# Moving phi off GpSimd, a four-bank PSUM tile for k^T v and attention, and layer norms in later stages, in a four-layer linear-attention and GLU kernel

## Chip, cores and metric

One NeuronCore of a Trainium2 chip. The metric is the device time of one execution in microseconds (us). Both kernels compute the same outputs. Engines are named as in the profile: PE is TensorE, PEld its weight loads, DVE is VectorE, ACT is ScalarE, POOL is GpSimd, SP is SyncE (here: the queue that issues all DMAs).

## The reference, cut to what matters

```python
def _A_ref(x, wqkv, wo):                       # H = 32 heads of 32
    q, k, v = split_heads(x @ wqkv)            # cut
    phi = lambda t: jnp.where(t > 0, t + 1, jnp.exp(t)) + 1e-6
    pq, pk = phi(q), phi(k)
    kv = jnp.einsum("bhsd,bhse->bhde", pk, v)  # needs all of k, v first
    z  = jnp.einsum("bhsd->bhd", pk)
    num = jnp.einsum("bhqd,bhde->bhqe", pq, kv)
    den = jnp.einsum("bhqd,bhd->bhq", pq, z)[..., None] + 1e-6
    return merge_heads(num / den) @ wo
def _B_ref(x, w_gate, w_up, w_down):
    return ((x @ w_gate) * (x @ w_up)) @ w_down
# x: 2048 x 1024, F = 3584, bf16
x = x + _A_ref(_layernorm(x), ...)   # A0
x = x + _B_ref(_layernorm(x), ...)   # B1
x = x + _A_ref(_layernorm(x), ...)   # A2
x = x + _B_ref(_layernorm(x), ...)   # B3
```

## The kernel before: the parts that matter

The author fixes the order of units; each engine runs its own instructions in that order. A token tile is 128 tokens; four tiles make a group. A layer norm is a *statistics* unit (DVE, then two tiny POOL operations for the reciprocal root), a *normalise* unit (DVE), and a *transpose* unit (eight PE transposes, one ACT copy). `weave(main, fill, first, step)` puts one fill unit after each `step` main units from `first` on, and **appends whatever is left of `fill` at the end**.

```python
def phi(ps, dst):                                   # once per 128x512 tile of k or q
    e = work.tile([P, NB], F32, tag="e", name="e")
    nc.scalar.activation(out=e[:], in_=ps[:], func=ACT.Exp)
    nc.gpsimd.tensor_scalar(out=e[:], in0=e[:], scalar1=1.0, scalar2=1e-6, op0=ALU.min, op1=ALU.add)
    nc.vector.scalar_tensor_tensor(out=dst, in0=ps[:], scalar=1.0 + 1e-6, in1=e[:], op0=ALU.add, op1=ALU.max)

def o_unit(t):                                      # attention of one token tile
    for chunks in BANKS:                            # 3 + 3 + 2 chunks of 128 columns, one bank each
        ps = aux_tile()                             # 3 one-bank buffers
        # ... one 132-column matmul per chunk ...
        nc.vector.tensor_scalar(out=den[:], in0=view[:, :, P:ZW], scalar1=1e-6, scalar2=None, op0=ALU.add)
        nc.vector.reciprocal(out=den[:], in_=den[:])
        nc.vector.tensor_tensor(out=onat..., in0=view[:, :, 0:P]..., in1=den[:]..., op=ALU.mult)

# start of layer A0
do([apply_unit(0), tx(0, 0), stats_unit(2), k_unit(0, 0), apply_unit(1), tx(1, 0), stats_unit(3),
    k_unit(1, 0), apply_unit(2), tx(2, 0), k_unit(2, 0), apply_unit(3), tx(3, 0), k_unit(3, 0)])

# attention and output stage: out_group(g) is, per tile, two output units and the statistics
do(weave([q_unit(2, c) for c in range(KD)], o_group(0), 1, 2))
do(weave([q_unit(3, c) for c in range(KD)], to_group(0), 0, 2))
do(weave(out_group(0), o_group(1) + to_group(1), 0, 1))     # four attention units, then four transposes
do(weave(out_group(1), o_group(2) + to_group(2), 0, 1))
do(weave(out_group(2), o_group(3) + to_group(3), 0, 1))
do(weave(out_group(3), ln0, 0, 1))
```

The kernel splits PSUM into eight one-bank buffers: four for matmuls, three auxiliary ones, one for transposes.

Of the kernel before, what the change touches and what calls it, by code (L numbers as in the profile page):

```python
# [25 lines left out]
def kernel(  # L26
# [22 lines left out]
    FB = F // NB  # L49
    HC = P // 32  # L50
    ZW = P + HC
    CPB = NB // ZW
    BANKS = [list(range(b, min(b + CPB, KD))) for b in range(0, KD, CPB)]

# [3 lines left out]
    small = ctx.enter_context(tc.tile_pool(name="small", bufs=NT + 2))  # L58
# [15 lines left out]
    onat = [H[:, o0 + i * D:o0 + (i + 1) * D] for i in range(4)]  # L74
    oT = [H[:, i * KD * G:(i + 1) * KD * G].rearrange("p (c s) -> p c s", s=G) for i in range(2)]
# [43 lines left out]
    for t in range(TPG):  # L119
        load(X[:, t, :], x_view[:, t, :])  # L120
    load_k(0)
# [22 lines left out]


    stat = {}

    def ln_stats(t):
# [3 lines left out]
        mv = small.tile([P, 2], F32, tag="mv", name="mv")  # L152
# [3 lines left out]
        rstd = small.tile([P, 1], F32, tag="rstd", name="rstd")  # L156
# [30 lines left out]
    def mm_tile():  # L187
        return psum.tile([P, NB], F32, tag="mm", bufs=4, name="ps")

    def aux_tile():  # L190
        return psum.tile([P, NB], F32, tag="aux", bufs=3, name="aux")

    def phi(ps, dst):

        e = work.tile([P, NB], F32, tag="e", name="e")
        nc.scalar.activation(out=e[:], in_=ps[:], func=ACT.Exp)  # L196
        nc.gpsimd.tensor_scalar(out=e[:], in0=e[:], scalar1=1.0, scalar2=1e-6, op0=ALU.min, op1=ALU.add)  # L197
        nc.vector.scalar_tensor_tensor(out=dst, in0=ps[:], scalar=1.0 + 1e-6, in1=e[:], op0=ALU.add, op1=ALU.max)  # L198
# [25 lines left out]
    def kv_unit(t):  # L224

        def run():
            if t == 0:
                acc[:] = [aux_tile() for _ in BANKS]
            for b, chunks in enumerate(BANKS):
                for j, c in enumerate(chunks):  # L230
                    nc.tensor.matmul(out=acc[b][:, j * ZW:(j + 1) * ZW], lhsT=pk[t % 4][:, c * P:(c + 1) * P],  # L231
                                     rhs=vz[t % 4][:, c, :], start=(t == 0 and j == 0),
                                     stop=(t == NT - 1), skip_group_check=True)
            if t == NT - 1:
                for b, chunks in enumerate(BANKS):
                    n = len(chunks)
                    nc.vector.tensor_tensor(
                        out=KVz[:, chunks[0]:chunks[0] + n, :],
                        in0=acc[b][:, 0:n * ZW].rearrange("p (c f) -> p c f", f=ZW),
                        in1=mask[:].unsqueeze(1).to_broadcast([P, n, ZW]), op=ALU.mult)  # L240
        return run
# [11 lines left out]
    def o_unit(t):  # L253

        def run():
            g, tl = t // TPG, t % TPG
            for chunks in BANKS:
                n = len(chunks)
                ps = aux_tile()
                for j, c in enumerate(chunks):  # L260
                    nc.tensor.matmul(out=ps[:, j * ZW:(j + 1) * ZW], lhsT=pqT[g % 3][:, c, tl * P:(tl + 1) * P],
                                     rhs=KVz[:, c, :], start=True, stop=True)
                view = ps[:, 0:n * ZW].rearrange("p (c f) -> p c f", f=ZW)
                den = small.tile([P, n, HC], F32, tag=f"den{n}", name="den")
                nc.vector.tensor_scalar(out=den[:], in0=view[:, :, P:ZW], scalar1=1e-6, scalar2=None, op0=ALU.add)
                nc.vector.reciprocal(out=den[:], in_=den[:])  # L266
                nc.vector.tensor_tensor(  # L267
                    out=onat[tl][:, chunks[0] * P:(chunks[0] + n) * P].rearrange("p (c h e) -> p c h e", c=n, h=HC),
                    in0=view[:, :, 0:P].rearrange("p c (h e) -> p c h e", h=HC),
                    in1=den[:].unsqueeze(3).to_broadcast([P, n, HC, 32]), op=ALU.mult)  # L270
        return run
# [21 lines left out]
    def gu_unit(i, f):  # L293
# [3 lines left out]
        def run():  # L297
# [6 lines left out]
            gs = work.tile([P, NB], F32, tag="e", name="gs")  # L304
# [4 lines left out]
    def d_unit(t, n, last):  # L309
        def run():  # L310
            ps = aux_tile()
# [28 lines left out]

    def ones():
        for i in range(4):
            nc.gpsimd.memset(vz[i][:, :, P:ZW], 1.0)

    def layer_A(li):
        ones()
        if li == 0:
            ln_stats(0)
            ln_stats(1)
            do([apply_unit(0), tx(0, 0), stats_unit(2), k_unit(0, 0), apply_unit(1), tx(1, 0), stats_unit(3),  # L350
                k_unit(1, 0), apply_unit(2), tx(2, 0), k_unit(2, 0), apply_unit(3), tx(3, 0), k_unit(3, 0)])
# [6 lines left out]
            lns = []  # L358
            for t in range(TPG, 2 * TPG):
                lns += [stats_unit(t), apply_unit(t)]  # L360
            do(weave(main, lns + tx_group(1, 1), 0, 1))
        else:
            fill = []
            for t in range(3 * TPG, NT):
                fill += [apply_unit(t), tx(t, 3)]
            do(weave(kv_group(0), fill, 0, 2))

# [3 lines left out]
        def next_ln(g):  # L371
            return stats_apply(g) + tx_group(g, g) if li == 0 else []
# [108 lines left out]
```

## Time and profile before

1807.2 us (median of 4 runs). I cut the profiled run into stages at the issue of marker matmuls in PE's timeline; the *floor* of a stage is its matmul counts times the warm issue times read there: 0.216 us for a 512-column matmul, 0.45 us for eight transposes, 0.47 us for eight 132-column matmuls. *Warm* means matmuls at full clock, *cold* at half; the *granted clock* is what the profile records of it.

| stage | us | floor |
|---|---|---|
| start of A0, to the first v matmul | 51.0 | 16 |
| A0 rest of k, v, half of q ("kvq0") | 155.0 | 137 |
| A0 rest of q, attention, output ("O0") | 131.1 | 99 |
| B1 to its last down-projection | 593.8 | 591 |
| turn: to the first k matmul of A2 | 5.5 | |
| A2 k, v, half of q ("kvq2") | 152.8 | 147 with the turn |
| A2 attention, output ("O2") | 130.6 | 99 |
| B3 | 585.7 | 586 |

The GLU layers run within 3 us of their floor; the loss is in the attention layers. The first lines below are from the page of the kernel before: PE's busy share, the granted clock in 40 equal slices of the span (tenths of full speed), and the chain of work that ended last, where POOL has a share.

```profile
PE 1707.1 (94%) x8535; PEld 804.7 (44%) x8704; DVE 527.6 (29%) x1030; ACT 341.7 (19%) x514; POOL 300.2 (17%) x280
...
PEclk6999998999999999999999999899999999999999
...
PE 83%; POOL 8%; DVE 6%; ACT 1%; issue 1%; DMA 0%; another core or an unknown queue 0%; SPq 0%; ACTq 0%
```

PE's waits of the kernel before (what it waited for, us in total, times, longest) name the culprits: the normalise (`xn`), the division (`aux L261 <- DVE H L267`) and the last step of phi (`L198`; 3.2 us more of it stand before v matmuls), all on DVE.

```profile
PE pt L172 <- DVE xn L165: 32.9, 17, 6.9
PE aux L261 <- DVE H L267: 27.8, 46, 1.3
PE ps L206 <- DVE H L198: 8.3, 4, 3.3
```

The timeline of one tile in the start of the kernel before (start, duration, engine, line, operation; in brackets the idle time before it and what ended it). Exp, POOL, DVE, normalise and transpose follow each other, PE waits 3.9 us, and its eight matmuls take 3.60 us, where eight take 1.89 at full clock:

```profile
20.29 3.60 PE L206 MATMUL ps<-W_74,xT_70 128*128 128x512 bf16 x8 [1.10 <-ACT xT_70 L173]
...
23.93 0.60 ACT L196 ACTIVATE e<-ps 128x512 f32<-128x512 f32 x1 [3.69 <-PE ps L206]
24.61 1.94 POOL L197 TENSOR_SCALAR e<-e 128x512 f32<-128x512 f32 x1 [4.11 <-ACT e L196]
26.59 0.69 DVE L198 SCALAR_TENSOR_TENSOR H<-ps,e 128x512 bf16<-128x512 f32 x1 [7.05 <-POOL e L197]
27.19 0.54 DVE L165 TENSOR_SCALAR xn<-X,mv,rstd 128x1024 bf16<-128x1024 bf16 x1
27.79 1.03 PE L172 MATMUL pt<-ident,xn 128*128 128x128 bf16 x8 [3.90 <-DVE xn L165]
```

And PE in the attention and output stage of the kernel before, where attention units (L261, each three banks) wait for DVE bank by bank:

```profile
245.36 1.89 PE L288 MATMUL ps<-D_79,H 128*128 128x512 bf16 x7
248.56 0.35 PE L261 MATMUL aux<-KVz,D_81 128*128 128x132 bf16 x3 [1.31 <-DVE H L267]
249.49 0.35 PE L261 MATMUL aux<-KVz,D_81 128*128 128x132 bf16 x3 [0.58 <-DVE H L267]
250.25 0.40 PE L261 MATMUL aux<-KVz,D_81 128*128 128x132 bf16 x2 [0.42 <-DVE H L267]
251.78 0.51 PE L261 MATMUL aux<-KVz,D_81 128*128 128x132 bf16 x3 [1.13 <-DVE H L267]
252.71 0.51 PE L261 MATMUL aux<-KVz,D_81 128*128 128x132 bf16 x3 [0.42 <-DVE H L267]
253.48 0.40 PE L261 MATMUL aux<-KVz,D_81 128*128 128x132 bf16 x2 [0.26 <-DVE H L267]
253.68 3.47 PE L288 MATMUL ps<-D_78,H 128*128 128x512 bf16 x8
```

The last line shows the second cost: after that stretch the next eight matmuls take 3.47 us instead of 1.89 (durations include the end of the pipeline), because the granted clock has fallen to half.

### The profile page before, as it was taken

The numbers are of one execution on the slowest core, as the hardware profiler recorded it, in microseconds if no ns is written. First come the engines' busy times: TensorE is split into PE (matmuls) and PEld (weight loads), VectorE is DVE, ScalarE is ACT, GpSimd is POOL, SyncE is SP. The second block draws the span as 40 slices with busy tenths as digits, with TensorE's granted clock in tenths as the row PEclk, the third lists the DMA queues.
The fourth block names the chain that finished last, engine by engine and source line by source line (L and its number), as shares of the span: only waits on it lengthen the run. The fifth ranks groups of instructions, "written<-read, shape, count | busy, mean of one in ns | idle before, by whom it ended". The sixth has DMA issues, their size and how long they took to land.

```text
span 1808.9 us, 20106 instructions
## 1 busy us (share of the span) xinstructions
PE 1707.1 (94%) x8535; PEld 804.7 (44%) x8704; DVE 527.6 (29%) x1030; ACT 341.7 (19%) x514; POOL 300.2 (17%) x280
## 2 busy tenths in 40 slices
PE   4889987999999999999989999789999999999999
PEld 1444444444444444444444444444444444444444
DVE  2333368422211221122122225872211111111111
ACT  1333221221111011012123333112101111110110
POOL 2466641100000000000014677110000000000000
PEclk6999998999999999999999999899999999999999
DMA  8000210544045035124120003008413431440500
GB/s 278 1 1 1 93 47 1 198 151 140 0 143 169 15 106 169 51 90 143 47 94 1 1 10 128 4 10 279 154 61 100 142 105 59 140 145 18 163 23 24
DMA packets 147514, 158.59 MB, mean 88 GB/s; under 512 B 3040, under 2 KB 138208, under 8 KB 147424
## 3 DMA queue, kind: packets, MB, share of 16 engines
q1 hardware_dynamic: 147424, 157.30, 26.6%
q8 instruction: 68, 1.11, 0.3%
q14 instruction: 22, 0.18, 0.0%
HBM read 153.09 MB, written 4.19 MB: 87 GB/s over the span
## 4 chain that ended last, share of the span: by engine, by line
PE 83%; POOL 8%; DVE 6%; ACT 1%; issue 1%; DMA 0%; another core or an unknown queue 0%; SPq 0%; ACTq 0%
PE ps L302 43%; PE aux L314 21%; POOL e L197 8%; PE ps L206 5%; PE ps L288 5%; PE ps L216 5%; PE pt L172 2%; DVE H L267 2%; PE ps L248 1%; DVE st L151 1%; DVE X L280 1%; DVE den L266 1%; PE aux L231 1%; DVE H L198 1%; ACT e L196 1%
## 5 line engine op out<-in xcount | busy, mean ns | idle before, releaser
L306 DVE TENSOR_TENSOR H<-gs,ps 128x512 bf16<-128x512 f32 x224 | 154.0, 687 | 613.7 <-PE ps L302 610.9
L197 POOL TENSOR_SCALAR e<-e 128x512 f32<-128x512 f32 x128 | 245.8, 1920 | 143.4 <-ACT e L196 136.4
L305 ACT COPY gs<-ps 128x512 f32<-128x512 f32 x224 | 131.2, 585 | 731.4 <-PE ps L302 705.6
L314 PEld LDWEIGHTS <-H 128*128 128x128 bf16 x1792 | 174.2, 98 | 207.3
L155 POOL TENSOR_SCALAR ve<-mv 128x1 f32<-128x1 f32 x64 | 15.8, 247 | 773.2 <-DVE mv L153 728.0
L280 DVE TENSOR_TENSOR X<-X,aux 128x512 bf16<-128x512 bf16 x64 | 44.0, 688 | 328.2 <-PE aux L314 312.2
L196 ACT ACTIVATE e<-ps 128x512 f32<-128x512 f32 x128 | 76.4, 597 | 179.9 <-PE ps L206 93.6
L198 DVE SCALAR_TENSOR_TENSOR H<-ps,e 128x512 bf16<-128x512 f32 x64 | 44.3, 692 | 193.4 <-POOL e L197 193.4
L302 PEld LDWEIGHTS <-W_75 128*128 128x128 bf16 x640 | 62.5, 98 | 75.7
L302 PEld LDWEIGHTS <-W_74 128*128 128x128 bf16 x640 | 62.4, 98 | 74.9
L302 PEld LDWEIGHTS <-W_77 128*128 128x128 bf16 x576 | 56.2, 98 | 68.1
L302 PEld LDWEIGHTS <-xT_73 128*128 128x128 bf16 x576 | 56.2, 98 | 68.1
L302 PEld LDWEIGHTS <-xT_72 128*128 128x128 bf16 x576 | 56.1, 98 | 67.1
L302 PEld LDWEIGHTS <-W_76 128*128 128x128 bf16 x576 | 56.0, 98 | 66.4
L151 DVE BATCH_NORM_STATS2 st<-X 128x6 f32<-128x512 bf16 x128 | 81.7, 680 | 3.5 <-DMA X<-in_A_x_dram 3.5
L302 PE MATMUL ps<-xT_71,W_75 128*128 128x512 bf16 x317 | 75.4, 379 | 0.3
L302 PE MATMUL ps<-xT_70,W_75 128*128 128x512 bf16 x318 | 75.5, 379 | 0.2
L288 PEld LDWEIGHTS <-H 128*128 128x128 bf16 x512 | 50.8, 103 | 55.9 <-issue 10.1
L302 PE MATMUL ps<-xT_70,xT_72 128*128 128x512 bf16 x316 | 75.4, 379 | 0.2
L302 PE MATMUL ps<-xT_70,xT_73 128*128 128x512 bf16 x312 | 74.8, 379 | 0.4
L302 PE MATMUL ps<-xT_71,W_76 128*128 128x512 bf16 x314 | 75.0, 379 | 0.3
L302 PE MATMUL ps<-xT_70,W_74 128*128 128x512 bf16 x310 | 74.8, 379 | 0.4
(91 smaller groups left out, 2082.4 us busy)
## 6 DMA issues: line engine op xcount, KB each, us to landing
W_74<-in_B_w_gate_dram SPq DMA_DIRECT2D x20, 1024.0 KB, 5.2
W_75<-in_B_w_up_dram SPq DMA_DIRECT2D x20, 1024.0 KB, 7.0
W_76<-in_B_w_gate_dram SPq DMA_DIRECT2D x18, 1024.0 KB, 5.2
W_77<-in_B_w_up_dram SPq DMA_DIRECT2D x18, 1024.0 KB, 7.2
xT_72<-in_B_w_gate_dram SPq DMA_DIRECT2D x18, 1024.0 KB, 5.2
xT_73<-in_B_w_up_dram SPq DMA_DIRECT2D x18, 1024.0 KB, 7.0
X<-in_A_x_dram SPq DMA_DIRECT2D x16, 256.0 KB, 7.6
out_dram<-X SPq DMA_DIRECT2D x32, 128.0 KB, 1.7
```

The lines of the kernel that those rows point to most:

```text
L151: nc.vector.bn_stats(out=st[:, c, :], in_=X[:, t, c * NB:(c + 1) * NB])
L196: nc.scalar.activation(out=e[:], in_=ps[:], func=ACT.Exp)
L197: nc.gpsimd.tensor_scalar(out=e[:], in0=e[:], scalar1=1.0, scalar2=1e-6, op0=ALU.min, op1=ALU.add)
L198: nc.vector.scalar_tensor_tensor(out=dst, in0=ps[:], scalar=1.0 + 1e-6, in1=e[:], op0=ALU.add, op1=ALU.max)
L206: nc.tensor.matmul(out=ps[:], lhsT=xt[:, k, tl * P:(tl + 1) * P], rhs=wk[n][:, k, :], start=(k == 0), stop=(k == KD - 1))
L216: nc.tensor.matmul(out=ps[:], lhsT=xt[:, k, tl * P:(tl + 1) * P], rhs=wv[n][:, k, :], start=(k == 0), stop=(k == KD - 1))
L280: nc.vector.tensor_tensor(out=X[:, t, n * NB:(n + 1) * NB], in0=X[:, t, n * NB:(n + 1) * NB], in1=ps[:], op=ALU.add)
L288: nc.tensor.matmul(out=ps[:], lhsT=oT[(t // TPG) % 2][:, c, tl * P:(tl + 1) * P], rhs=wo[n][:, c, :], start=(c == 0), stop=(c == KD - 1))
L302: nc.tensor.matmul(out=ps[:], lhsT=w[:, k, j * P:(j + 1) * P], rhs=xT[g % 2][:, k, :], start=(k == 0), stop=(k == KD - 1))
L305: nc.scalar.copy(out=gs[:], in_=gp[:])
L306: nc.vector.tensor_tensor(out=hT[:, f, :], in0=gs[:], in1=up[:], op=ALU.mult)
L314: nc.tensor.matmul(out=ps[:], lhsT=hT[:, f, tl * P:(tl + 1) * P], rhs=wd[f][:, n * NB:(n + 1) * NB], start=(f == 0), stop=(f == KF - 1))
```

## The change

Intent: take POOL out of phi, make the division three DVE operations per tile instead of nine, take layer-norm work out of stages where DVE is busy, shorten the start. PSUM is split anew: three matmul buffers, one four-bank tile, one bank for transposes. Core of the diff (cut):

```diff
-    for t in range(TPG): load(X[:, t, :], x_view[:, t, :])
-    load_k(0)
+    # x tiles 0 and 1, the first k half in two parts, x tiles 2 and 3, then the rest
+    nc.vector.memset(xT[3][:, 0, :], 0.0)
+    for i in range(16):                                # zero matmuls
+        nc.tensor.matmul(out=zps[:], lhsT=xT[3][:, 0, 0:P], rhs=xT[3][:, 0, :], start=True, stop=True)
 def phi(ps, dst):
-        e = work.tile([P, NB], F32, tag="e", name="e")
-        nc.gpsimd.tensor_scalar(out=e[:], in0=e[:], scalar1=1.0, scalar2=1e-6, op0=ALU.min, op1=ALU.add)
+        e = eb[phis[0] % 3]                            # bf16, three buffers
+        nc.vector.tensor_scalar(out=e, in0=e, scalar1=1.0, scalar2=1e-6, op0=ALU.min, op1=ALU.add)
 def o_unit(t):
-            for chunks in BANKS:                       # three banks, nine DVE operations
+            ps = kv_tile()                             # [P, 8, 256] fp32, four banks, one buffer
+            # eight matmuls, then ONE add, ONE reciprocal, ONE multiply over all eight chunks
 def layer_A(li):                                       # start: all norms ahead of the phis on DVE
+            for t in range(TPG):
+                ln_stats(t)
+                if t > 0: ln_apply(t - 1)
+            ln_apply(3)
+            for t in range(TPG):
+                tx(t, 0)()
+                k_unit(t, 0)()
-        return [... (out_unit(t, 0), out_unit(t, 1), stats_unit(t))]
+        return [... (out_unit(t, 0), out_unit(t, 1))]
-        do(weave(out_group(0), o_group(1) + to_group(1), 0, 1))      # o o o o t t t t
+            return [o[0], o[1], tr[0], o[2], tr[1], o[3], tr[2], tr[3]]   # o_fill(g)
+        do(weave(out_group(0), o_fill(1), 0, 1))
+        do(weave(out_group(1), [stats_unit(t) for t in range(TPG)] + o_fill(2), 0, 1))
 def layer_B(li):                                       # statistics come with the norms, in gate/up stages
+            if g == 3 and not last:
+                fill = norm_fill(1, 1, True) + norm_fill(2, 2, True)    # 24 units into 12 places
```

In the k/v/q stage of A0 the norms of the next group now come as four statistics in a row, then normalises and transposes.

More of the change, by code (lines that the diff above doesn't have):

```diff
@@ L49 @@
     FB = F // NB
+    MM = 3
     HC = P // 32
     ZW = P + HC
-    CPB = NB // ZW
-    BANKS = [list(range(b, min(b + CPB, KD))) for b in range(0, KD, CPB)]
+    ZS = NB // 2
     ctx.enter_context(tc.manual_schedule())
@@ L57 @@
     work = ctx.enter_context(tc.tile_pool(name="work", bufs=4))
-    small = ctx.enter_context(tc.tile_pool(name="small", bufs=NT + 2))
+    small = ctx.enter_context(tc.tile_pool(name="small", bufs=4))
     psum = ctx.enter_context(tc.tile_pool(name="psum", bufs=1, space=bass.MemoryType.PSUM))
@@ L74 @@
     onat = [H[:, o0 + i * D:o0 + (i + 1) * D] for i in range(4)]
+    o0 += 4 * D
+    eb = [H[:, o0 + i * NB:o0 + (i + 1) * NB] for i in range(3)]
     oT = [H[:, i * KD * G:(i + 1) * KD * G].rearrange("p (c s) -> p c s", s=G) for i in range(2)]
@@ L117, in load_d @@
             load(Dr[i][:].rearrange("p (f n) -> p f n", n=D), wd_v[:, 4 * i:4 * i + 4, :])
-    for t in range(TPG):
-        load(X[:, t, :], x_view[:, t, :])
-    load_k(0)
+    load(X[:, 0, :], x_view[:, 0, :])
+    load(X[:, 1, :], x_view[:, 1, :])
+    for k in range(0, KD, 4):
+        load(wk[0][:, k:k + 4, :], wqkv_v[:, k:k + 4, D:D + NB])
+    load(X[:, 2, :], x_view[:, 2, :])
+    load(X[:, 3, :], x_view[:, 3, :])
     load_k(1)
@@ L143 @@
     nc.scalar.activation(out=warm[:], in_=mhalf[:], func=ACT.Exp)
+    nc.vector.memset(xT[3][:, 0, :], 0.0)
+    zps = psum.tile([P, NB], F32, tag="mm", bufs=MM, name="zps")
+    for i in range(16):
+        nc.tensor.matmul(out=zps[:], lhsT=xT[3][:, 0, 0:P], rhs=xT[3][:, 0, :], start=True, stop=True)
     stat = {}
@@ L151, in ln_stats @@
             nc.vector.bn_stats(out=st[:, c, :], in_=X[:, t, c * NB:(c + 1) * NB])
-        mv = small.tile([P, 2], F32, tag="mv", name="mv")
+        mv = small.tile([P, 2], F32, tag="mv", bufs=2 * TPG, name="mv")
         nc.vector.bn_aggr(out=mv[:], in_=st[:])
@@ L155, in ln_stats @@
         nc.gpsimd.tensor_scalar(out=ve[:], in0=mv[:, 1:2], scalar1=1e-5, scalar2=None, op0=ALU.add)
-        rstd = small.tile([P, 1], F32, tag="rstd", name="rstd")
+        rstd = small.tile([P, 1], F32, tag="rstd", bufs=2 * TPG, name="rstd")
         nc.gpsimd.tensor_tensor(out=rstd[:], in0=ve[:], in1=mhalf[:], op=ALU.pow)
@@ L187, in mm_tile, with kv_tile @@
     def mm_tile():
-        return psum.tile([P, NB], F32, tag="mm", bufs=4, name="ps")
-    def aux_tile():
-        return psum.tile([P, NB], F32, tag="aux", bufs=3, name="aux")
+        return psum.tile([P, NB], F32, tag="mm", bufs=MM, name="ps")
+    def kv_tile():
+        return psum.tile([P, KD, ZS], F32, tag="kv", bufs=1, name="kv")
+    phis = [0]
     def phi(ps, dst):
-        e = work.tile([P, NB], F32, tag="e", name="e")
-        nc.scalar.activation(out=e[:], in_=ps[:], func=ACT.Exp)
-        nc.gpsimd.tensor_scalar(out=e[:], in0=e[:], scalar1=1.0, scalar2=1e-6, op0=ALU.min, op1=ALU.add)
-        nc.vector.scalar_tensor_tensor(out=dst, in0=ps[:], scalar=1.0 + 1e-6, in1=e[:], op0=ALU.add, op1=ALU.max)
+        e = eb[phis[0] % 3]
+        phis[0] += 1
+        nc.scalar.activation(out=e, in_=ps[:], func=ACT.Exp)
+        nc.vector.tensor_scalar(out=e, in0=e, scalar1=1.0, scalar2=1e-6, op0=ALU.min, op1=ALU.add)
+        nc.vector.scalar_tensor_tensor(out=dst, in0=ps[:], scalar=1.0 + 1e-6, in1=e, op0=ALU.add, op1=ALU.max)
     def k_unit(t, n):
@@ L227, in run @@
             if t == 0:
-                acc[:] = [aux_tile() for _ in BANKS]
-            for b, chunks in enumerate(BANKS):
-                for j, c in enumerate(chunks):
-                    nc.tensor.matmul(out=acc[b][:, j * ZW:(j + 1) * ZW], lhsT=pk[t % 4][:, c * P:(c + 1) * P],
-                                     rhs=vz[t % 4][:, c, :], start=(t == 0 and j == 0),
-                                     stop=(t == NT - 1), skip_group_check=True)
-            if t == NT - 1:
-                for b, chunks in enumerate(BANKS):
-                    n = len(chunks)
-                    nc.vector.tensor_tensor(
-                        out=KVz[:, chunks[0]:chunks[0] + n, :],
-                        in0=acc[b][:, 0:n * ZW].rearrange("p (c f) -> p c f", f=ZW),
-                        in1=mask[:].unsqueeze(1).to_broadcast([P, n, ZW]), op=ALU.mult)
+                acc[:] = [kv_tile()]
+            for c in range(KD):
+                nc.tensor.matmul(out=acc[0][:, c, 0:ZW], lhsT=pk[t % 4][:, c * P:(c + 1) * P],
+                                 rhs=vz[t % 4][:, c, :], start=(t == 0 and c % 2 == 0),
+                                 stop=(t == NT - 1), skip_group_check=True)
+            if t == NT - 1:
+                nc.vector.tensor_tensor(out=KVz[:], in0=acc[0][:, :, 0:ZW],
+                                        in1=mask[:].unsqueeze(1).to_broadcast([P, KD, ZW]), op=ALU.mult)
         return run
@@ L256, in run @@
             g, tl = t // TPG, t % TPG
-            for chunks in BANKS:
-                n = len(chunks)
-                ps = aux_tile()
-                for j, c in enumerate(chunks):
-                    nc.tensor.matmul(out=ps[:, j * ZW:(j + 1) * ZW], lhsT=pqT[g % 3][:, c, tl * P:(tl + 1) * P],
-                                     rhs=KVz[:, c, :], start=True, stop=True)
-                view = ps[:, 0:n * ZW].rearrange("p (c f) -> p c f", f=ZW)
-                den = small.tile([P, n, HC], F32, tag=f"den{n}", name="den")
-                nc.vector.tensor_scalar(out=den[:], in0=view[:, :, P:ZW], scalar1=1e-6, scalar2=None, op0=ALU.add)
-                nc.vector.reciprocal(out=den[:], in_=den[:])
-                nc.vector.tensor_tensor(
-                    out=onat[tl][:, chunks[0] * P:(chunks[0] + n) * P].rearrange("p (c h e) -> p c h e", c=n, h=HC),
-                    in0=view[:, :, 0:P].rearrange("p c (h e) -> p c h e", h=HC),
-                    in1=den[:].unsqueeze(3).to_broadcast([P, n, HC, 32]), op=ALU.mult)
+            ps = kv_tile()
+            for c in range(KD):
+                nc.tensor.matmul(out=ps[:, c, 0:ZW], lhsT=pqT[g % 3][:, c, tl * P:(tl + 1) * P],
+                                 rhs=KVz[:, c, :], start=True, stop=True)
+            den = small.tile([P, KD, HC], F32, tag="den", name="den")
+            nc.vector.tensor_scalar(out=den[:], in0=ps[:, :, P:ZW], scalar1=1e-6, scalar2=None, op0=ALU.add)
+            nc.vector.reciprocal(out=den[:], in_=den[:])
+            nc.vector.tensor_tensor(
+                out=onat[tl].rearrange("p (c h e) -> p c h e", c=KD, h=HC),
+                in0=ps[:, :, 0:P].rearrange("p c (h e) -> p c h e", h=HC),
+                in1=den[:].unsqueeze(3).to_broadcast([P, KD, HC, 32]), op=ALU.mult)
         return run
@@ L303, in run @@
                                      start=(k == 0), stop=(k == KD - 1))
-            gs = work.tile([P, NB], F32, tag="e", name="gs")
+            gs = work.tile([P, NB], F32, tag="gs", name="gs", bufs=3)
             nc.scalar.copy(out=gs[:], in_=gp[:])
@@ L310, in run @@
         def run():
-            ps = aux_tile()
+            ps = mm_tile()
             tl = t % TPG
@@ L339, in kv_group, with q_group @@
         return units
+    def q_group(g):
+        return [q_unit(g, c) for c in range(KD)]
     def ones():
@@ L343, in ones, with norm_fill @@
             nc.gpsimd.memset(vz[i][:, :, P:ZW], 1.0)
+    def norm_fill(g, slot, stats):
+        ts = range(g * TPG, (g + 1) * TPG)
+        st = [stats_unit(t) for t in ts] if stats else []
+        ap = [apply_unit(t) for t in ts]
+        tr = [tx(t, slot) for t in ts]
+        return st + [ap[0], ap[1], tr[0], ap[2], tr[1], ap[3], tr[2], tr[3]]
     def layer_A(li):
@@ L347, in layer_A @@
         if li == 0:
-            ln_stats(0)
-            ln_stats(1)
-            do([apply_unit(0), tx(0, 0), stats_unit(2), k_unit(0, 0), apply_unit(1), tx(1, 0), stats_unit(3),
-                k_unit(1, 0), apply_unit(2), tx(2, 0), k_unit(2, 0), apply_unit(3), tx(3, 0), k_unit(3, 0)])
+            for t in range(TPG):
+                ln_stats(t)
+                if t > 0:
+                    ln_apply(t - 1)
+            ln_apply(3)
+            for t in range(TPG):
+                tx(t, 0)()
+                k_unit(t, 0)()
             ts = range(TPG)
@@ L357, in layer_A @@
                     main.append(kv_unit(t - 1))
-            lns = []
-            for t in range(TPG, 2 * TPG):
-                lns += [stats_unit(t), apply_unit(t)]
-            do(weave(main, lns + tx_group(1, 1), 0, 1))
-        else:
-            fill = []
-            for t in range(3 * TPG, NT):
-                fill += [apply_unit(t), tx(t, 3)]
-            do(weave(kv_group(0), fill, 0, 2))
-        def stats_apply(g):
-            return [u for t in range(g * TPG, (g + 1) * TPG) for u in (stats_unit(t), apply_unit(t))]
-        def next_ln(g):
-            return stats_apply(g) + tx_group(g, g) if li == 0 else []
-        do(weave(kv_group(1), next_ln(2), 0, 1))
-        do([q_unit(0, c) for c in range(KD)])
-        do(weave(kv_group(2), next_ln(3), 0, 1))
-        do([q_unit(1, c) for c in range(KD)])
+            do(weave(main, norm_fill(1, 1, True), 1, 1))
+        else:
+            do(weave(kv_group(0), norm_fill(3, 3, False), 1, 2))
+        do(weave(kv_group(1), norm_fill(2, 2, True) if li == 0 else [], 1, 1))
+        do(q_group(0))
+        do(weave(kv_group(2), norm_fill(3, 3, True) if li == 0 else [], 1, 1))
+        do(q_group(1))
         do(kv_group(3) + [kv_unit(NT - 1)])
@@ L380, in layer_A, with o_fill @@
         load_gu(1)
-        def o_group(g):
-            return [o_unit(t) for t in range(g * TPG, (g + 1) * TPG)]
-        def to_group(g):
-            return [to_unit(t) for t in range(g * TPG, (g + 1) * TPG)]
+        def o_fill(g):
+            o = [o_unit(t) for t in range(g * TPG, (g + 1) * TPG)]
+            tr = [to_unit(t) for t in range(g * TPG, (g + 1) * TPG)]
+            return [o[0], o[1], tr[0], o[2], tr[1], o[3], tr[2], tr[3]]
         def out_group(g):
-            return [u for t in range(g * TPG, (g + 1) * TPG)
-                    for u in (out_unit(t, 0), out_unit(t, 1), stats_unit(t))]
-        do(weave([q_unit(2, c) for c in range(KD)], o_group(0), 1, 2))
-        do(weave([q_unit(3, c) for c in range(KD)], to_group(0), 0, 2))
+            return [u for t in range(g * TPG, (g + 1) * TPG) for u in (out_unit(t, 0), out_unit(t, 1))]
+        f0 = o_fill(0)
+        do(weave(q_group(2), [f0[i] for i in (0, 1, 3, 5)], 1, 2))
+        do(weave(q_group(3), [f0[i] for i in (2, 4, 6, 7)], 0, 2))
         load_gu(2)
-        ln0 = [u for t in range(TPG) for u in (apply_unit(t), tx(t, 0))]
-        do(weave(out_group(0), o_group(1) + to_group(1), 0, 1))
-        do(weave(out_group(1), o_group(2) + to_group(2), 0, 1))
-        do(weave(out_group(2), o_group(3) + to_group(3), 0, 1))
-        do(weave(out_group(3), ln0, 0, 1))
+        do(weave(out_group(0), o_fill(1), 0, 1))
+        do(weave(out_group(1), [stats_unit(t) for t in range(TPG)] + o_fill(2), 0, 1))
+        do(weave(out_group(2), o_fill(3), 0, 1))
+        do(weave(out_group(3), norm_fill(0, 0, False), 0, 1))
     def layer_B(li):
+        last = li == 3
         load_d()
-        nxt = [u for t in range(TPG, 2 * TPG) for u in (apply_unit(t), tx(t, 1))]
-        last = li == 3
+        nxt = norm_fill(1, 1, True)
         for g in range(NG):
@@ L410, in layer_B @@
                 main.append(prefetch(i, last))
-            do(weave(main, nxt if g < 2 or not last else [], 4, 2))
+            do(weave(main, nxt, 2, 1))
             nxt = []
@@ L416, in layer_B @@
                 main += [d_unit(t, 0, last), d_unit(t, 1, last)]
-                if not last:
+                if g == NG - 1 and not last:
                     main.append(stats_unit(t))
-            fill = []
-            if g + 2 < NG:
-                for t in range((g + 2) * TPG, (g + 3) * TPG):
-                    fill += [apply_unit(t), tx(t, g % 2)]
-            elif g == 2 and not last:
-                nxt = [u for t in range(TPG) for u in (apply_unit(t), tx(t, 0))]
-            elif g == 3 and not last:
-                for gg in (1, 2):
-                    for t in range(gg * TPG, (gg + 1) * TPG):
-                        fill += [apply_unit(t), tx(t, gg)]
+            if g == 0:
+                nxt = norm_fill(2, 0, True)
+            elif g == 1:
+                nxt = norm_fill(3, 1, True)
+            elif g == 2 and not last:
+                nxt = norm_fill(0, 0, True)
+            fill = []
+            if g == 3 and not last:
+                fill = norm_fill(1, 1, True) + norm_fill(2, 2, True)
             do(weave(main, fill, 0, 1))
```

## The prediction

> **What bounds it now.** TensorE: 94% busy on the page; the chain that ended last is 83% PE, 8% POOL, 6% DVE. In the timeline a warm 512-column matmul takes 0.216 us, eight transposes 0.45, eight 132-column matmuls 0.47. Times the counts: floors of 252 us (first attention layer A0), 591 (first GLU layer B1), 247 (A2), 586 (B3). Measured: 337, 594, 289, 589. The loss (85 + 42 us) is in the attention layers:
> - Start, 0 to 50.8 us, floor 16: the first four tiles run transpose, copy, matmuls, exp, POOL, DVE, next norm in series; granted clock 0.50 from 20 to 40 us. Loss 35.
> - A0 k/v/q, 51 to 206: loss 18; PE waits 11.5 us (wait table) for the DVE half of phi, behind POOL's 1.92 us a tile (matmuls: 1.73).
> - Attention and output projection, 131 us per attention layer, floor 99: loss 32, of which 14 are waits for the DVE division and about 12 a dropped clock (0.66 to 0.87 in ten-us windows). DVE is 83% busy: nine small operations a tile (3.2 us), two adds (0.68 each), statistics (1.5).
> - A2 k/v/q: loss 12, mostly at the change of layer.
>
> **What the change does.**
> 1. phi: POOL's 1.92 us becomes a DVE bf16 operation; the 1024-wide bf16 normalise takes 0.55, so about 0.3. DVE needs 1.0 us of each 1.73; nothing binds. The Trainium skill, "GPSIMD Engine Reference", Key points, calls DVE about 2x faster for elementwise work; I expect more (bf16). A0 k/v/q: gain 15.
> 2. Division: three operations a tile. Extrapolating 557 ns (384 elements) and 424 (256): 1.2 us for 1024, 1.6 in all instead of 3.2. Statistics leave this stage except four. But one buffer serializes neighbouring tiles: about 0.5 us waits in two groups; in the second output group four statistics (6 us) and four units left after the weave make about 4.5; the last transpose before B 1.3. Loss 8 instead of 32, clock 1.0: gain 24 per attention layer.
> 3. Start: two x tiles, half weights; norms before phis. First matmul near 9 us, 3.4 us a tile, V matmuls from about 28 instead of 50.8. "TensorE: Matmul & The Clock Gate", Part 1, says about 3.4 us of activity releases the clock; the trace agrees (slow until about 45 us, when matmuls become dense). The zero matmuls should do that before data arrives, if 64% duty keeps it. Gain 19 (23 warm, 10 cold).
> 4. Norms in B: DVE has room (20% busy); removes about 3 us of waits. Three matmul buffers are enough.
> 5. New cost: at the end of B1, twelve norm units follow the last down-projection; five statistics (7.5 us) lie ahead of the first normalise on DVE; k starts 14 to 17 us after, instead of 5.4, partly at half clock. Loss 6 to 9 more.
>
> **Sum.** 19 + 15 + 48 + 3 - 7 = 78, less a few us for unseen waits: 1807.5 - 76 = 1731 us; 8 in 10: 1718 to 1750. Chances: faster by over 2% 0.96; same 0.035; slower 0.005.
>
> **What would show it.** First V matmul near 28 us, clock 1.0 before; no POOL in the chain; attention and output stage about 107 us at clock 1.0; a hole of 10 us or more at B1 to A2, PE waiting for DVE xn; B layers 591 and 588.
>
> **What would make it wrong.** Clock staying at half in the start; the 4-bank read slower than 1.04 ns an element, or one buffer stalling every tile; the bf16 step at full width (0.6 us); waits for matmul buffers in B.

## The result, and the profile after

1729.0 us (median of 4 runs), 0.957 of before (95% interval 0.955 to 0.959). The forecast was 1731.

| stage | before | after | gain | forecast gain |
|---|---|---|---|---|
| start | 51.0 | 28.5 | 22.5 | 19 (23 warm, 10 cold) |
| kvq0 | 155.0 | 142.7 | 12.4 | 15 |
| O0 | 131.1 | 106.6 | 24.5 | 24 |
| B1 | 593.8 | 588.2 | 5.6 | 3 with B3 |
| turn and kvq2 | 158.3 | 165.7 | -7.3 | -6 to -9 |
| O2 | 130.6 | 106.6 | 24.0 | 24 |
| B3 | 585.7 | 585.7 | 0.0 | |

The gains add to about 81.6 us, against 78.2 between the medians: the profiled run of before was 3 us slower than its median. The same views as before. From the page of the changed kernel, POOL has left the chain:

```profile
PE 1680.1 (97%) x8550; PEld 802.9 (46%) x8720; DVE 538.8 (31%) x963; ACT 341.3 (20%) x514; POOL 54.0 (3%) x152
...
PEclk9999999999999999999989999999999999999999
...
PE 95%; DVE 3%; ACT 1%; issue 1%; DMA 0%; SPq 0%; DVEq 0%; ACTq 0%
```

PE's waits after the change. The normalise fell from 32.9 to 8.8 us, of which 6.0 is one wait, and the division from 27.8 to 7.4 plus 3.0:

```profile
PE pt L182 <- DVE xn L175: 8.8, 5, 6.0
PE kv L267 <- DVE H L272: 7.4, 8, 1.6
...
PE pt L182 <- DVE H L272: 3.0, 2, 1.5
```

The start in the timeline of the changed kernel: the zero matmuls, then for each tile transpose, copy (the wait for ACT) and eight matmuls at full clock. L229 is the first v matmul:

```profile
1.18 5.54 PE L153 MATMUL zps<-xT_73 128*128 128x512 bf16 x16 [1.18 <-DVE xT_73 L150]
...
12.88 1.90 PE L219 MATMUL ps<-W_74,xT_70 128*128 128x512 bf16 x8 [1.10 <-ACT xT_70 L183]
14.61 0.61 PE L182 MATMUL pt<-ident,xn 128*128 128x128 bf16 x8
...
28.51 7.07 PE L229 MATMUL ps<-W_76,xT_70 128*128 128x512 bf16 x32
```

The attention and output stage of the changed kernel, in its worst place, the second output group with its four statistics and the units that the weave left over. Three waits of 1.4 to 1.6 us are what remains; the forecast said "about 4.5":

```profile
232.81 0.64 PE L267 MATMUL kv<-KVz,D_82 128*128 128x132 bf16 x8 [1.39 <-DVE H L272]
...
239.88 0.64 PE L267 MATMUL kv<-KVz,D_82 128*128 128x132 bf16 x8 [1.62 <-DVE H L272]
240.36 0.61 PE L182 MATMUL pt<-ident,H 128*128 128x128 bf16 x8
242.46 0.62 PE L182 MATMUL pt<-ident,H 128*128 128x128 bf16 x8 [1.49 <-DVE H L272]
```

And the new hole at the turn: a 6.05 us wait for a normalise, four transposes in single file at half clock (1.0 us instead of 0.6), then k 15.5 us after the down-projections ended:

```profile
867.66 0.61 PE L182 MATMUL pt<-ident,xn 128*128 128x128 bf16 x8 [1.10 <-ACT xT_71 L183]
874.32 1.04 PE L182 MATMUL pt<-ident,xn 128*128 128x128 bf16 x8 [6.05 <-DVE xn L175]
...
880.67 1.01 PE L182 MATMUL pt<-ident,xn 128*128 128x128 bf16 x8 [1.10 <-ACT xT_72 L183]
881.48 0.63 PE L219 MATMUL ps<-W_74,xT_70 128*128 128x512 bf16 x1
```

The sum matches. The question for the experiments is whether it matches for the reasons given.

### The profile page after: what moved, and what is told of

It is laid out like the page before. It is cut to its first block, busy times and chain, and to the rows that moved or that the text cites. A ratio compares the mean times of both kernels' runs of the same rounds, so it can differ in the third digit from the quotient of the medians.

```text
span 1727.3 us, 19979 instructions
## 1 busy us (share of the span) xinstructions
PE 1680.1 (97%) x8550; PEld 802.9 (46%) x8720; DVE 538.8 (31%) x963; ACT 341.3 (20%) x514; POOL 54.0 (3%) x152
## 4 chain that ended last, share of the span: by engine, by line
PE 95%; DVE 3%; ACT 1%; issue 1%; DMA 0%; SPq 0%; DVEq 0%; ACTq 0%
PE ps L307 45%; PE ps L319 22%; PE ps L229 6%; PE ps L256 6%; PE ps L219 6%; PE ps L293 5%; PE pt L182 2%; DVE st L161 1%; PE kv L243 1%; PE kv L267 1%; DVE H L272 1%; DVE X L285 1%; DMA X<-in_A_x_dram 0%; ACT xT_70 L183 0%; ACT xT_72 L183 0%
## 5 line engine op out<-in xcount | busy, mean ns | idle before, releaser
L285 DVE TENSOR_TENSOR X<-X,ps 128x512 bf16<-128x512 bf16 x128 | 87.4, 683 | 375.4 <-PE ps L319 331.3
L209 ACT ACTIVATE H<-ps 128x512 bf16<-128x512 f32 x128 | 76.4, 597 | 149.7 <-PE ps L256 71.0
L210 DVE TENSOR_SCALAR H<-H 128x512 bf16<-128x512 bf16 x128 | 37.3, 291 | 199.3 <-ACT H L209 199.3
L307 PE MATMUL ps<-xT_70,W_74 128*128 128x512 bf16 x312 | 75.2, 379 | 2.7 <-ACT xT_70 L183 2.2
L307 PE MATMUL ps<-xT_71,W_76 128*128 128x512 bf16 x313 | 75.2, 379 | 0.4
L307 PE MATMUL ps<-xT_71,W_74 128*128 128x512 bf16 x312 | 75.2, 379 | 0.5
L307 PE MATMUL ps<-xT_70,xT_72 128*128 128x512 bf16 x312 | 75.2, 379 | 0.4
L307 PE MATMUL ps<-xT_71,W_75 128*128 128x512 bf16 x315 | 75.2, 379 | 0.2
L307 PE MATMUL ps<-xT_71,W_77 128*128 128x512 bf16 x315 | 75.0, 379 | 0.2
L307 PE MATMUL ps<-xT_70,W_75 128*128 128x512 bf16 x316 | 75.1, 379 | 0.1
L307 PE MATMUL ps<-xT_70,xT_73 128*128 128x512 bf16 x314 | 75.0, 379 | 0.2
```

Of the source, the lines that this page charges most:

```text
L209: nc.scalar.activation(out=e, in_=ps[:], func=ACT.Exp)
L210: nc.vector.tensor_scalar(out=e, in0=e, scalar1=1.0, scalar2=1e-6, op0=ALU.min, op1=ALU.add)
L285: nc.vector.tensor_tensor(out=X[:, t, n * NB:(n + 1) * NB], in0=X[:, t, n * NB:(n + 1) * NB], in1=ps[:], op=ALU.add)
L307: nc.tensor.matmul(out=ps[:], lhsT=w[:, k, j * P:(j + 1) * P], rhs=xT[g % 2][:, k, :], start=(k == 0), stop=(k == KD - 1))
```

## The experiments

All twelve are the *changed* kernel with the edit named (three of them combine several edits); all gave right results. "Effect" is the run's ratio to before minus the changed kernel's ratio (0.9569), times 1807.5 us; with intervals of about plus or minus 0.0015 on each ratio, effects under about 4 us are not to be trusted. The stages, from one profile each, repeat better (kvq0 was 142.6 to 142.7 in nine kernels whose edit does not touch it). The start does not: V matmuls began between 28.1 and 31.5 us in the seven kernels that have the changed start and phi unedited. In the late ones the third x tile arrived later: in f1_turn its statistics began at 10.6 instead of 9.2 us, the clock fell for one tile (3.48 us for its eight matmuls), and V began at 31.5. The output stage, too, took 106.6 in most kernels that leave it alone, but 109.0 and 108.3 in the profile of r5_old_order, the slowest of its four runs, and 108.2 once in f3_start.

| run | edit | us | effect | stage that moved |
|---|---|---|---|---|
| r1_no_zero | no zero matmuls | 1730.2 | +0.7 | V at 30.0 |
| r5_old_order | old order of the start | 1740.5 | +11.4 | V at 40.7 |
| r2_phi_pool | phi step on GpSimd | 1773.5 | +44.5 | kvq0 168.0, kvq2 154.3, O 111.7 |
| r6_phi_f32 | phi step in fp32 | 1731.2 | +0.7 | kvq0 143.2 |
| r3_split_div | nine division operations | 1749.0 | +18.6 | O 115.9, 116.2 |
| r4_stats_out | statistics back in O | 1732.4 | +2.2 | O 104.4; B1 592.0, B3 589.5 |
| r34_both | both | 1752.5 | +23.0 | O 114.1 |
| r7_old_stage | both, old unit order | 1778.7 | +47.9 | O 126.9, 126.8 |
| f1_turn | repair of the turn | 1719.1 | -10.5 | turn 0.0, B1 594.7 |
| f2_out | repair of O | 1717.7 | -12.7 | O 100.8 |
| f3_start | repair of the start | 1728.0 | -2.0 | V at 24.7, kvq0 145.6 |
| f4_all | all three repairs | 1704.2 | -25.8 | O 100.8, turn 0.0, V 24.6 |

### The start: zero matmuls or order

```diff
-    nc.vector.memset(xT[3][:, 0, :], 0.0)
-    zps = psum.tile(...); for i in range(16): nc.tensor.matmul(...)
```

> The changed kernel without its 16 zero matmuls (and their memset). Theory A (the zero matmuls keep the whole start at full clock): the start runs at half clock until the second half of the k weights, V matmuls begin near 41 us instead of 28.5, time 1739 to 1743. Rival B (the denser order of the start would release the clock by itself, and the zero matmuls save only the first few us): V matmuls from 31 to 34 us, time 1731 to 1735.

Measured: 1730.2 us, V matmuls at 30.0. My theory A fell; rival B, which expected V from 31 us, was nearer. The timeline of this run shows only the first transposes and eight matmuls cold, the next eight already at full speed; the clock was released by the real work. (The granted clock on record reads 1.00 all this time, from 8 to 12 us too, so here only the durations show the cold start.)

```profile
8.94 3.60 PE L215 MATMUL ps<-W,xT 128*128 128x512 bf16 x8 [1.10 <-ACT xT L179]
...
14.38 1.90 PE L215 MATMUL ps<-W,xT 128*128 128x512 bf16 x8 [1.10 <-ACT xT L179]
```

The zero matmuls are worth at most the 1.5 us seen here, and that lies inside the start's own spread.

The counterpart keeps the zero matmuls and takes the old order:

```diff
-            for t in range(TPG): ln_stats(t); ...           # norms first
+            do([apply_unit(0), tx(0, 0), stats_unit(2), k_unit(0, 0), apply_unit(1), tx(1, 0), ...])
```

> The changed kernel with the old order of norms, transposes and k matmuls for the first four tiles (phi ahead of the next norm on DVE), zero matmuls and new loads kept. Theory A (the zero matmuls are not enough: the clock stays up only if the order keeps TensorE over about half busy; here 2.2 us of each 5.6): the clock falls back to half, V matmuls from 40 to 45 us, time 1740 to 1746. Rival B (once released the clock stays; the order only shortens the chain by about 2 us a tile): V matmuls near 34 us, time 1734 to 1737.

Measured: 1740.5 us, V at 40.7: theory A. The clock fell back although the zero matmuls had released it; each tile took 5.9 to 7.5 us instead of 3.5 to 4.3. Windows of this run (length, busy us of PE, PEld, DVE, ACT, POOL with counts, granted clock, DMA share, GB/s):

```profile
5.00:10.00 5.00, 3.38 (x22) 1.54 (x21) 1.93 (x6) 1.01 (x1) 1.77 (x4) 1.00 1.00 334
...
15.00:20.00 5.00, 3.04 (x8) 0.73 (x5) 1.26 (x3) 0.60 (x1) 0.13 (x1) 0.70 1.09 362
...
30.00:35.00 5.00, 5.00 (x13) 1.81 (x12) 0.98 (x2) 0.60 (x1) 0.00 (x0) 0.50 1.07 369
```

So 12 of the 22.5 us come from the order of the norms. The other 10 (51.0 to 40.7) are the shorter phi, the loads and the zero matmuls together. About 2 of them are the loads: the first k matmul starts at 8.61 us in this run and at 10.69 in the kernel before, where it waits 2.8 us for its weights. I did not separate the rest.

### phi: which engine, which type

```diff
-        nc.vector.tensor_scalar(out=e, in0=e, scalar1=1.0, scalar2=1e-6, op0=ALU.min, op1=ALU.add)
+        nc.gpsimd.tensor_scalar(out=e, in0=e, scalar1=1.0, scalar2=1e-6, op0=ALU.min, op1=ALU.add)
```

> The changed kernel with the middle step of phi on GpSimd again (bf16 in place), all else kept. Theory A (POOL's 1.92 us a tile against 1.73 of matmuls is what held the k/v/q stages, worse with three buffers than with four): the k/v/q stages of both attention layers grow, the first from 142.7 to 152 to 160 us, time 1740 to 1755, with GpSimd back in the chain. Rival B (the gain of 12 us there came from where the norms stand on DVE, not from GpSimd): under 3 us, time 1728 to 1732.

Measured: 1773.5 us. Right direction, but far above the range. Where no norm statistics run among the phis (kvq2), POOL costs 4.1 us; in each O stage 5.1; in kvq0, where they do, 25.3, twice the whole gain of the change there. (The profile is of the fastest of the four runs, 1769.7 us; its stages explain 40 us.) The timeline of this run shows why:

```profile
62.90 0.60 ACT L209 ACTIVATE H<-ps 128x512 bf16<-128x512 f32 x1 [1.09 <-PE ps L219]
...
66.90 0.57 POOL L167 TENSOR_TENSOR rstd<-ve,mhalf 128x1 f32<-128x1 f32 x1
67.55 3.96 POOL L210 TENSOR_SCALAR H<-H 128x512 bf16<-128x512 bf16 x2
69.53 0.69 DVE L211 SCALAR_TENSOR_TENSOR H<-ps,H 128x512 bf16<-128x512 f32 x1 [3.02 <-POOL H L210]
70.13 0.54 DVE L175 TENSOR_SCALAR xn<-X,mv,rstd 128x1024 bf16<-128x1024 bf16 x1
70.73 1.03 PE L182 MATMUL pt<-ident,xn 128*128 128x128 bf16 x8 [5.67 <-DVE xn L175]
```

Exp is done by 63.5, but POOL takes it only at 67.6: ahead of it in POOL's order stand the four reciprocal roots, each of which waits for statistics on DVE. The statistics in turn had waited for the last step of the phis before, which waited for POOL. DVE and POOL hold each other up through their fixed orders, and PE waits 5.67 us for the normalise behind it. The new order of the norms needs phi off POOL; the two parts of the change belong together.

```diff
-        e = eb[phis[0] % 3]          # bf16
+        e = work.tile([P, NB], F32, tag="gs", name="e", bufs=3)[:]
```

> The changed kernel with phi's intermediate in fp32 instead of bf16, middle step on VectorE. The step will take 0.3 to 0.6 us instead of 0.29, DVE at most 1.3 of each 1.73 us of matmuls, so it should not bind: time 1728 to 1731. If bf16 matters on the critical path (three matmul buffers held longer, kv matmuls waiting for phi): 1733 or more.

Measured: 1731.2 us, no effect clear of noise; the step took 424 ns instead of 291. kvq0 grew by 0.5 us. With the step on DVE, fp32 would have done as well; bf16 is not what brought the time.

### The attention and output stage

```diff
+            for c0, n in ((0, 3), (3, 3), (6, 2)):    # same four-bank tile
                 # add, reciprocal, multiply on chunks c0 to c0 + n
```

> The changed kernel with the division of a tile split again into 3 + 3 + 2 chunks (nine DVE operations, about 3.2 us a tile instead of 1.8), still on the one four-bank tile. Theory A (the gain of 24 us per attention and output stage is the halved DVE time of the division, with one buffer holding it): each stage grows from 106.6 to 114 to 120 us, time 1744 to 1756. Rival B (it is the statistics having left the stage): each stage grows by under 3 us, time under 1735.

Measured: 1749.0 us, stages of 115.9 and 116.2: theory A, 9.4 us a stage.

```diff
-  for u in (out_unit(t, 0), out_unit(t, 1))
+  for u in (out_unit(t, 0), out_unit(t, 1), stats_unit(t))   # and no statistics in B for these norms
-        do(weave(out_group(1), [stats_unit(t) for t in range(TPG)] + o_fill(2), 0, 1))
+        do(weave(out_group(1), o_fill(2), 0, 1))
```

> The changed kernel with the statistics of each tile back in the attention and output stage, behind its two output units (DVE then 4.7 us a tile against about 4.4 of TensorE). Theory A: each stage grows by 2 to 6 us (108 to 113), time 1733 to 1741. Rival B (the statistics were the main cost): each stage 120 us or more, time over 1755.

Measured: 1732.4 us, and both theories were wrong: the stage became *shorter*, 104.4 us instead of 106.6. With the fast division DVE copes with one statistics unit per tile; what costs more is four of them bunched in one group, with units left over after it. PE's waits in the output groups of A0 account for the 2.2 us: 4.1 us for the division instead of 5.2, and the 1.1 for the last transpose before B is gone. The time did not fall because B1 and B3 grew by 3.8 us each. There, without statistics between them, the transposes follow each other and wait for the one transpose buffer (in PE's waits 13 such waits with 13.0 us in all, against 7 with 6.5 in the changed kernel).

> Both of the above: split division and statistics in the stage, on one four-bank tile. If the two costs are DVE time and add once DVE is saturated (6.1 us a tile against 4.4), the stage is 130 us or more, like before (131), time 1775 to 1790, and the clock drops below 0.9 in some ten-us windows. If the stage stays under 120, the three-buffer PSUM layout of before was itself a part of its 131 us.

Measured: 1752.5 us, stages of 114.1: under 120, against expectation. 131.1 minus 114.1 leaves 17 us that neither the number of division operations nor the statistics explain. The expectation names PSUM's layout as the reason for such a result, but I had also left the *order* of the units out, so I tested that:

```diff
-            return [o[0], o[1], tr[0], o[2], tr[1], o[3], tr[2], tr[3]]
+            return o + tr                      # on top of r34_both; likewise in the q stages
+        # last group: normalise and transpose of each tile in turn, as before (instead of norm_fill)
```

> The changed kernel with the attention and output stage as it was in the old one but for the four-bank tile and the engine of phi: split division, statistics in the stage, and the old order of units (four attention units in a row, then four transposes). The kernel with the first two alone had stages of 114.1 us, where the old kernel has 131, and GpSimd's phi is worth 5.1 of the rest. Theory A (the order of the units, which I had not priced, is most of what is left: attention units one output unit apart wait for each other's division): stages of 122 to 127 us, time 1768 to 1780, clock below 0.9 in some ten-us windows. Rival B (the three one-bank tiles of before were the rest): under 117 us, time under 1759.

Measured: 1778.7 us, stages of 126.9 and 126.8, the clock at 0.77 to 0.89 in four ten-us windows: the size of theory A, so the order is the cause. Its mechanism is only a part of it. The whole difference to r34_both lies in the output groups (93.9 us against 81.1 in A0). PE's waits there: for the division 12.7 us in 6 waits, against 11.5 in 9; for the one transpose buffer 3.5, against none; for normalises in the last group, whose old order this edit restored too, 1.7, against none. That is 6.4 of the 12.8 us. The other 6.4 are matmuls at a lower clock (0.93 on average against 1.00): the same waiting, bunched, seems to cost the clock.

Adding the 5.1 us of POOL's phi gives 132.0, against 131.1 in the kernel before; nothing is left for PSUM's layout, if those 5.1 us, measured on the changed kernel, hold for the old order too. (The output groups alone took 93.9 us in both.) In the timeline of this run, the second attention unit stands one output unit (1.73 us) behind the first and waits 1.23 us. Between the second and the third there is only a statistics unit, nothing for PE, and the third waits 2.82 us:

```profile
209.30 1.89 PE L294 MATMUL ps<-D,H 128*128 128x512 bf16 x8
212.41 0.64 PE L267 MATMUL kv<-KVz,D 128*128 128x132 bf16 x8 [1.23 <-DVE H L273]
215.87 1.06 PE L267 MATMUL kv<-KVz,D 128*128 128x132 bf16 x8 [2.82 <-DVE H L273]
216.73 3.04 PE L294 MATMUL ps<-D,H 128*128 128x512 bf16 x8
```

The eight matmuls of the last line take 3.04 us: waits of this size also cost the clock. In r34_both, the same place has a transpose and an output unit between second and third, the third waits 0.65 us, and the clock stays at 1.00:

```profile
210.35 0.64 PE L267 MATMUL kv<-KVz,D 128*128 128x132 bf16 x8 [1.22 <-DVE H L273]
210.82 0.61 PE L182 MATMUL pt<-ident,H 128*128 128x128 bf16 x8
211.27 1.89 PE L294 MATMUL ps<-D,H 128*128 128x512 bf16 x8
213.80 0.64 PE L267 MATMUL kv<-KVz,D 128*128 128x132 bf16 x8 [0.65 <-DVE H L273]
```

### The repairs

f1_turn: the statistics of tiles 4 to 11 go into the last gate/up stage, where DVE is mostly idle (one to two tenths busy in the page's slices), and the remaining units are paired so that none is left over.

```diff
-                nxt = norm_fill(0, 0, True)
+                nxt = norm_fill(0, 0, True) + [stats_unit(t) for t in range(TPG, 3 * TPG)]
-                fill = norm_fill(1, 1, True) + norm_fill(2, 2, True)
+                fill = [...]   # normalise t+1 and transpose t as one unit: 9 units in 12 places
```

> The changed kernel with the norm statistics of tiles 4 to 11 moved into the last gate/up stage of the first GLU layer, and the remaining normalise and transpose units paired so that none is left after the last down-projection. If the 15.4 us between the last down-projection matmul and the first k matmul are DVE statistics in the wrong place, they shrink to under 1 us and the whole time falls by 11 to 14 us (to 1715 to 1718; 4 of the six transposes' 2.7 us stay, elsewhere). Rival: the wait is only replaced by one for the normalise or the single transpose buffer inside the down-projections: gain under 5 us.

Measured: 1719.1 us, effect -10.5. The turn is gone (15.5 to 0.0); B1 grew by 6.5: the six transposes cost 2.7 in their new places, and three of them wait there for the transpose buffer (3.3 us).

f2_out: statistics two by two with the last two fill units of the second and third group; the last transpose before B one place earlier.

```diff
-        do(weave(out_group(1), [stats_unit(t) for t in range(TPG)] + o_fill(2), 0, 1))
-        do(weave(out_group(2), o_fill(3), 0, 1))
+        do(weave(out_group(1), with_stats(o_fill(2), 0, 1), 0, 1))
+        do(weave(out_group(2), with_stats(o_fill(3), 2, 3), 0, 1))
```

> The changed kernel with the four statistics spread two by two over the second and third output groups, no unit left after a group, and the last transpose ahead of the last output unit. If the 4.5 us of waits in the second group and the 1.1 before the GLU layer come from those places, each attention and output stage shrinks from 106.6 to 101 to 102 us and the time to 1718 to 1721. Rival: DVE is late anyway and the waits move to the next group: under 4 us gained.

Measured: 1717.7 us, stages of 100.8 against a floor of 99.

f3_start: two transposes ahead, matmuls of the second k half in between.

```diff
+            do([tx(0, 0), tx(1, 0), k_unit(0, 0), k_unit(1, 0), tx(2, 0), k_unit(0, 1), tx(3, 0), k_unit(1, 1), ...])
```

> The changed kernel with the first four tiles in another order: two transposes ahead, second-half k matmuls of early tiles in between, and the normalise of tile 1 ahead of the statistics of tile 2 on DVE. If the 3.4 us per tile of the start are the chain transpose, copy, matmul, V matmuls begin near 24 instead of 28.5 us, time 1723 to 1726. Rival: the loads of x and of the second k half set the pace, no gain (1727 to 1730).

Measured: 1728.0 us; the effect of -2.0 is not clear of noise. The start did shrink, to 24.7, as the first theory said. It was given back: the shorter unit list of the next stage leaves two transposes over, which wait for the single buffer, and kvq0 grew by 2.9 us; and in its profile the clock dropped for part of O0 (0.83 in one ten-us window, 1.6 us more).

> The changed kernel with the three repairs together (start order, statistics and leftovers of the output stage, statistics before the change of layer). If they sit at separate places the gains add: 5 + 9 + 12 = 26 us, time 1700 to 1706. If a repaired place exposes another limit (loads at the start, DVE in the last down-projections), 1708 or more.

Measured: 1704.2 us (median of 4 runs), 0.943 of before (0.941 to 0.944), 1.5% under the changed kernel. The three effects add to -25.2, the measured one is -25.8. The granted clock is 1.000 on average, PE is 98% busy. It beats both kernels.

## Why the prediction was right

The time was forecast within 2 us, and the places of gain and loss were right. Not every reason was, and the closeness of the sum is in part luck: the start gained 3.5 us more than forecast and B1 about 2.6 more, kvq0 2.6 less.

- *Bounds.* Right: floors, the loss per stage, GLU layers at the floor.
- *Step 1, phi.* 12.4 us instead of 15: direction right. "I expect more (bf16)" was beside the point: fp32 does as well (r6_phi_f32). POOL's rate, 1.92 against 1.73 us, is the small part: 4.1 us where there are no norms. The larger part seems to be the coupling of POOL's and DVE's orders through the norms, which the forecast did not see: in the kernel before, all six waits for the last step of phi (11.5 us) stand in kvq0, beside norm statistics, and kvq2, with the same POOL, has none. No run separates the two there; that the changed order would have made the coupling worse is shown (25.3 us in r2_phi_pool).
- *Step 2, division.* 24.5 and 24.0 forecast as 24, but the bookkeeping was wrong. The waits for the division and the dropped clock were named rightly as the loss; what removed them was not. The forecast named nine operations to three and "Statistics leave this stage". Measured along one path: POOL's phi about 5 us a stage, the order of the units 12.8 (126.9 to 114.1, half of it clock), the statistics *minus* 2.2 (104.4 to 106.6), nine operations to three 9.7 (114.1 to 104.4). The largest piece was not in the forecast, and one that it counted as a gain is a loss. These pieces were measured on one path; on another, for example the old unit order with the fast division, they may divide differently. The single durations were right: 1.22 us for the 1024-element multiply against "1.2".
- *Step 3, start.* V at 28.5 against "about 28". "The zero matmuls should do that" came true and hardly mattered: with them the first real matmuls run at full clock, but without them the clock is released at about the end of the first eight, 1.5 us lost at most where the forecast put 13 between warm and cold; and with them it still falls if the order leaves PE idle. The condition added there, "if 64% duty keeps it", was the part that mattered.
- *Step 4, norms in B.* Right in B1, which gained 5.6: three waits for the normalise (3.7 us, "about 3" forecast) are gone, and about 1.35 us are three transposes that moved behind the cut (six stand there now, three before). B3, 0.0.
- *Step 5, the turn.* Right: 15.5 us, "14 to 17" forecast, with the wait for `xn` as named; f1_turn confirms it.

## What to carry to other kernels

In a kernel whose order is fixed by hand, price the order of the units as carefully as the operations: two users of one buffer need enough other work between them to cover the first one's consumer (a unit without matmuls fills a place in the list but covers nothing), and a fill list longer than its places leaves a serial tail (f1_turn and f2_out removed such tails, and moved statistics, for 10 and 13 us). When one step moves to another engine, ask which tiny operations of others share that engine's queue. And a forecast that hits the sum is no proof of its terms: take each part away once before crediting it.

## What the Trainium skill lacked or had wrong

- "GPSIMD Engine Reference", Key points, puts VectorE at about twice GpSimd for elementwise work, and its Engine selection calls one-input operations roughly line-rate. Here the one-input 128x512 min-and-add took 1920 ns on GpSimd, in fp32 and in bf16 alike, against 424 ns (fp32) and 291 ns (bf16) on VectorE: 4.5 and 6.6 times.
- "TensorE: Matmul & The Clock Gate", Why this matters, asks for no idle gaps over about 3 us to keep the clock. Here it fell to half with no single gap over 1.31 us, in the stretch from 248.6 to 253.5 us of the kernel before, where PE was busy 2.64 of 6 us with short matmuls (windows view, 248 to 254). The page also names such micro-idling, under "A second HAM failure mode", but has no figure for the busy share. Here the clock fell at 44% (that stretch) and 43% (2.52 of 5.9 us, r5_old_order from 8.6) and held at 61% (4.87 of 8 us, the changed kernel from 8 to 16) and 68% (4.09 of 6 us, r34_both from 208).
- The same page, Part 1, gives about 3.4 us of activity for the release. That agrees at the start of two runs: zero operands count (16 zero matmuls took 5.54 us, between 16 cold at 0.43 and 16 warm at 0.216), and in r1_no_zero about the first eight real matmuls (3.60 us) were cold. It was not enough in the kernel before: eight matmuls in a row took 3.60 us and left the clock at half (from 20.29 and from 29.93 us); the release came at 45.4, 5.8 us after the matmuls had become dense. The page calls the ramp under 1% of a typical span; here a warm-up brought at most 1.5 us where the first real work is dense, and was lost again where it isn't (r5_old_order).
- The same page, Part 4, gives about 275 ns for a 128x128 transpose inside a kernel and says that the full clock does not engage for transposes. Here one lasts 226 ns on average in the kernel before, but eight in a row are issued in 0.45 us, and they take 0.61 us at full clock against 1.03 at half: they follow the granted clock as matmuls do, and the page lacks the rate of a stream. Whether transposes alone release the clock, no run shows.
